# Attention with two expert layers: the two heads of a pair on even and odd partitions

## The chip, the cores and the metric

The kernel runs on one core of one Trainium2 chip. The metric is the device time of one execution in microseconds (us). The engines are TensorE (PE in the profile; PEld is its weight load), VectorE (DVE), ScalarE (ACT), GpSimd (POOL) and SyncE (SP). SP and ACT issue nearly all transfers of the stage that is told of here.

## What is computed

Attention of two kinds over 4 batches of 8 heads, 576 positions and 64 dimensions, then two layers of experts:

```python
q_d, k_d, v_d = (mean over 4 neighbouring positions of q, k, v)     # 144 pooled positions
out_d = softmax(q_d k_d^T / 8) v_d ; out_up = repeat(out_d, 4)
mask = abs(pos[:, None] - pos[None, :]) < 4                         # local attention, 7 keys wide
out_local = softmax(where(mask, q k^T / 8, -1e9)) v
x = out_up + out_local                                              # [2304, 512]
x = moe(x)          # top 1 of 8 experts, only rows with x @ w_skip > 0, plus x
x = moe2(x)         # noisy top 2 of 8 experts
```

## The kernel before

**Tiles of the attention stage.** The 2304 rows are cut into 18 tiles of 128 rows (4 groups of 32 queries). For each tile, class `Local` makes scores, softmax and values of the local attention; between the tiles, class `Pooled` does the same for the pooled attention of a batch. `push` (lines 1044 to 1083) runs a unit's `scores` and `soft`, the `turn` of the unit two back, the steps due now (`later`), then `exp`, and the `values` of the unit three back. The order on TensorE, ACT, VectorE and GpSimd is that of the program here (line 599); SP's queue is ordered by the framework.

**Heads in pairs.** The 8 heads go in 4 pairs. The two heads of a pair share the 128 partitions: queries `qT` hold head 0 in partitions 0 to 63 and head 1 in 64 to 127. The key tile `kT` has two blocks, `kT[:, 0]` and `kT[:, 1]`; head 0's keys fill partitions 0 to 63 of block 0, head 1's fill 64 to 127 of block 1, and the other halves are zero (`zero_keys`, line 631), so that one matmul gives both heads' scores (line 913). There are two key tiles, for even and odd batches. `load_qk` (728) loads a batch's keys, head 0 on SP and head 1 on ACT, then its queries on SP. `pool_qk` (737) sums groups of four keys and queries into `kd` and `qd`; the zero halves of `kd` are filled by `zero_pooled_keys`.

**Local exponentials and values.** `soft` (918) takes the maximum and writes scores minus maximum into `e` [128, 8 heads, 64 columns], of which 38 are used and column 48 holds 1e-9; `exp` works on it in place, `turn` transposes two heads at a time (128 columns) into `eT`, so the columns of head 0 come to partitions 0 to 63. `values` (938) sums `e` per head, multiplies `eT` with the window values `vw`, and scales. `load_local` (847) loads a tile's window values, 48 partitions per head, head 0 to partitions 0 to 47 on SP, head 1 to 64 to 111 on ACT.

**The head of the program** (1090 to 1106) makes masks, fills the first key tile (half on VectorE, half on GpSimd), loads batch 0's keys and queries, and for three tiles fills `e` (GpSimd) and `vw` (ACT) and loads window values; then `load_v(0)` loads the batch's values on SP. `start_1` (695), due at tile 0, fills the second key tile on ACT, ahead of tile 0's exponentials; `start_2` (707), at tile 1, loads batch 1; `start_3` makes the other constants. At tile 3 `load_wall` (1109) loads the gate weights on SP, four small transfers; one step later VectorE copies them into `wall`. The steps after it on VectorE stand behind that copy.

**After the stage** comes routing and the first expert layer (matmuls at lines 545 and 558), then the second (1520 and 1535).

Of the kernel before, what the change touches and what calls it, by code (L numbers as in the profile page):

```python
# [10 lines left out]
F32 = mybir.dt.float32  # L11
# [4 lines left out]
OP = mybir.AluOpType  # L16
AX = mybir.AxisListType

B, H, S, D = 4, 8, 576, 64
N = B * S  # L20
DM = H * D
# [3 lines left out]
NPOOL = S // 4  # L25
QUARTERS = S // 32
W = 38
WV = 48
# [70 lines left out]
def moe_attention_kernel(ctx, tc, q, k, v, w_skip, w_gate, w1, w2, g2, n2, noise, u1, u2, out, dbg=None):  # L99
# [22 lines left out]
    def bank(tag, shape, dtype=F32):  # L122
        return psums[0].tile(shape, dtype, name=tag, tag=tag, bufs=psum_bufs[tag])


    rt = ctx.enter_context(tc.tile_pool(name="routing", bufs=1))
    jp = rt.tile([128, 128], F32, name="jp", tag="rows")
# [11 lines left out]
    sel = consts.tile([128, 32], F32, name="sel")  # L139


    shared = ctx.enter_context(tc.tile_pool(name="shared", bufs=1))
    early_ctx = ctx.enter_context(ExitStack())
    ep = early_ctx.enter_context(tc.tile_pool(name="early", bufs=1, side="right"))
    V = nc.vector
# [451 lines left out]
    with ExitStack() as actx:  # L597
# [11 lines left out]
        for i in range(WARM):  # L609
            nc.tensor.matmul(wp, warm[:, 0:128], warm, start=True, stop=True)  # L610

        def load_v(b):
            t = ld.tile([128, 4, DM], F32, name="v0", bufs=NVG)
            u = ld.tile([64, DM], F32, name="v1", bufs=NVG)
            r0 = b * S * DM
            nc.sync.dma_start(t, v[r0:r0 + 512 * DM].rearrange("(p c d) -> p c d", p=128, d=DM))
            nc.sync.dma_start(u, v[r0 + 512 * DM:r0 + S * DM].rearrange("(p d) -> p d", d=DM))
            return t, u

        vws, vds, es, eps, kTs, kds = [], [], [], [], [], []  # L620
# [7 lines left out]
            else:  # L628
                e.memset(t, value)

        def zero_keys(i, e0, e1):
            t = shared.tile([128, 2, 4, S], F32, name=f"kT{i}", bufs=1, tag=f"shared{i}")
            kTs.append(t)
            fill(e0, t[0:64, 1])
            fill(e1, t[64:128, 0])

        def zero_pooled_keys(i, e0, e1):
            t = at.tile([128, 4, 2, NPOOL], F32, name=f"kd{i}", bufs=1)
            fill(e0, t[0:64, :, 1, :])
            fill(e1, t[64:128, :, 0, :])  # L640
            kds.append(t)

        def zero_values(e):
            t = at.tile([128, 2, 4, 4 * D], F32, name=f"vw{len(vws)}", bufs=1)
# [2 lines left out]

        def zero_exps(e):

            t = at.tile([128, 8, 64], F32, name=f"e{len(es)}", bufs=1)  # L650
            fill(e, t)
            e.memset(t[:, :, EPS:EPS + 1], 1e-9)
            es.append(t)

        def zero_pooled_exps(e):
# [37 lines left out]
        offsets = [tuple(window(4 * t + s)[3] for s in range(4)) for t in range(NT)]  # L693
        V, P, A = nc.vector, nc.gpsimd, nc.scalar
        def start_1():
            zero_keys(1, A, A)
            for n in range(3, NES):
                zero_exps(P)
            for n in range(3, NVW):
                zero_values(P)  # L700
            pooled_ones(P)
            zero_pooled_exps(P)
            zero_pooled_exps(P)
            for d in offsets:
                distances(d)

        def start_2():
            for n in range(2, NEP):
                zero_pooled_exps(P)
            zero_pooled_keys(1, P, P)  # L710
            pooled_ones(P)
            nc.gpsimd.dma_start(x_d[0:1], kTs[1][0:1, 1, 0, 0:DM + 16])
            load_qk(1)
            for n in range(1, NVG):
                vgs[n] = load_v(n)
            for t in range(3, NVW):
                load_local(t)
# [10 lines left out]
        def load_qk(b):  # L728

            held["k", b % 2] = b  # L730
            qT[b] = at.tile([128, 4, S], F32, name="qT", bufs=2)
            for g in range(2):
                r = slice(64 * g, 64 * g + 64)
                (nc.sync, nc.scalar)[g].dma_start(kTs[b % 2][r, g], k[b, r])
            nc.sync.dma_start(qT[b], q[b])

        def pool_qk(b, n):


            assert held["k", b % 2] == b  # L740
            held["kd", b % 2] = (b, n)
            if n == 0:
                qd[b] = at.tile([128, 4, NPOOL], F32, name="qd", bufs=2)
            kd, kT = kds[b % 2], kTs[b % 2]
            if n >= 8 and b in ONDVE:
                for i in range(n - 8, 4, 3):
                    o, x = kd[64:128, i, 1], kT[64:128, 1, i]
                    nc.vector.tensor_reduce(o, x.rearrange("p (g r) -> p g r", r=4), axis=AX.X, op=OP.add)
            elif n < 8:
                i = n // 2  # L750
                o, x = (qd[b][:, i], qT[b][:, i]) if n % 2 == 0 else (kd[0:64, i, 0], kT[0:64, 0, i])
                nc.vector.tensor_reduce(o, x.rearrange("p (g r) -> p g r", r=4), axis=AX.X, op=OP.add)
            else:
                o, x = kd[64:128, :, 1], kT[64:128, 1].rearrange("p a (g r) -> p a g r", r=4)
                nc.gpsimd.tensor_tensor(o, x[:, :, :, 0] if n == 8 else o, x[:, :, :, n - 7], op=OP.add)

        def pool_v(b, n):
# [89 lines left out]
        def load_local(t):  # L847

            vw = vws[t % NVW]
            for g in range(2):  # L850
                o = N * DM + (2 * t + g) * WV * 1024
                (nc.sync, nc.scalar)[g].dma_start(vw[64 * g:64 * g + WV, g],
                                  v[o:o + WV * 1024].rearrange("(p s c) -> p s c", s=4, c=256))

        def load_up(t):
# [40 lines left out]
        class Local:  # L896
# [21 lines left out]
            def soft(self):  # L918
                mx = at.tile([128, 8], F32, name="mx", bufs=NES)
                nc.vector.tensor_reduce(mx, self.p, axis=AX.X, op=OP.max)  # L920
                self.e = es[self.tile_no % NES]
                e = self.e[:, :, 0:W]
                nc.vector.tensor_tensor(e, self.p, mx[:, :, None].to_broadcast([128, 8, W]), op=OP.subtract)

            def exp(self):
                e = self.e[:, :, 0:W]
                nc.scalar.activation(e, e, AF.Exp, scale=1.0 / math.sqrt(D))
                self.sums = at.tile([128, 8], F32, name="sums", bufs=4)

            def turn(self):  # L930
                p = bank("pT", [128, 4, 128])
                for i in range(4):
                    nc.tensor.transpose(p[:, i, :], self.e[:, 2 * i:2 * i + 2, :].rearrange("p g c -> p (g c)"),
                                        ident)
                self.eT = at.tile([128, 4, 128], F32, name="eT", bufs=NET)
                nc.scalar.activation(self.eT, p, AF.Copy)

            def values(self):
                t = self.tile_no
                nc.vector.tensor_reduce(self.sums, self.e[:, :, 0:EPS + 1], axis=AX.X, op=OP.add)  # L940
                nc.vector.reciprocal(self.sums, self.sums)
                p = bank("pB", [128, 4, 2, D])
                for i in range(4):
                    for s in range(4):
                        nc.tensor.matmul(p[s * 32:s * 32 + 32, i, :, :], self.eT[:, i, s * 32:s * 32 + 32],
                                         vws[t % NVW][:, :, s, i * D:i * D + D], start=True, stop=True,
                                         tile_position=(0, 32 * s), skip_group_check=True)
                x = at.tile([128, DM + 16], F32, name="x", bufs=XB)
                xs[t] = x
                nc.vector.tensor_tensor(x[:, 0:DM].rearrange("p (h d) -> p h d", d=D),  # L950
                                        p.rearrange("p i g d -> p (i g) d"),
                                        self.sums[:, :, None].to_broadcast([128, 8, D]), op=OP.mult)
# [135 lines left out]
            return window(4 * t + 3)[0]  # L1088

        vgs = {}  # L1090
        for d in offsets[0:2]:
            distances(d)
        mask(offsets[0])
        zero_keys(0, V, P)
        load_qk(0)
        mask(offsets[1])
        for t in range(3):
            zero_exps(P)
            zero_values(A)
            load_local(t)  # L1100
        zero_pooled_keys(0, P, P)
        vgs[0] = load_v(0)

        nc.vector.memset(wall, 0.0)
        nc.vector.tensor_reduce(fours, ident.rearrange("p (c k) -> p c k", k=4), axis=AX.X, op=OP.add)
# [739 lines left out]
def laid_out(name, a):  # L1845

    import numpy as np

    if name in ("q", "k"):
        a = a.reshape(B, 4, 2, S, D).transpose(0, 2, 4, 1, 3).reshape(B, 128, 4, S)  # L1850
# [30 lines left out]
```

## Time and profile before

| | before |
|---|---|
| median of 3 runs | 811.86 us (809.7 to 814.34) |
| the profiled execution, whole | 807.94 us |
| its span, first to last instruction | 805.8 us |
| TensorE busy | 763.1 us (95%) |
| VectorE busy | 359.5 us (45%) |
| ACT busy | 256.8 us (32%) |
| GpSimd busy | 237.4 us (29%) |

Times in the rows count from the start of the span. "Idle before" and the bracket behind an instruction name what ended the idle time of its engine. A busy share is an average over stages that have different limits; the attention stage lasts up to about 160 us, the rest is the two expert layers.

### The profile page before, as it was taken

To read this page: it belongs to the slowest core of one execution; us is meant where nothing else is said; L and a number is where in the kernel's file an instruction comes from. 1 tells how busy PE (TensorE), PEld (TensorE's weight loads), DVE (VectorE), ACT (ScalarE), POOL (GpSimd) and SP (SyncE) were. 2 spreads that over 40 slices of the span, in tenths; PEclk is the share of its full clock that TensorE was granted. 3 is DMA by queue.
4 is the path that set the end of the run, shared out by engine and by line. 5 is a ranking of instruction groups with operands and counts; after the bars stand their busy time and mean duration, and the time that the engine had idled before them with its cause. 6 is when DMAs were issued, how large, how long until landed. Compare 5 with 4: busy or idle time off the path is not lost.

```text
span 805.8 us, 15250 instructions
## 1 busy us (share of the span) xinstructions
PE 763.1 (95%) x6265; PEld 673.7 (84%) x6265; DVE 359.5 (45%) x814; ACT 256.8 (32%) x491; POOL 237.4 (29%) x242
## 2 busy tenths in 40 slices
PE   4789998799999999998999999999999999999996
PEld 2467686699999989997899899898898898997984
DVE  4797788441101256554965434244243243243210
ACT  6245453211111204322433533334233343342211
POOL 8204522032122353203345502403404305102012
PEclk9899999599999999999999999999999999999999
DMA  9999666759788986224263843724625526424113
GB/s 224 239 258 248 198 179 185 244 160 372 286 312 296 328 317 202 58 80 81 71 180 106 225 114 119 173 73 131 146 71 161 108 84 165 110 79 70 17 13 47
DMA packets 61402, 131.55 MB, mean 163 GB/s; under 512 B 16097, under 2 KB 17136, under 8 KB 59792
## 3 DMA queue, kind: packets, MB, share of 16 engines
q1 hardware_dynamic: 32320, 59.05, 25.1%
q10 hardware_dynamic: 17024, 45.48, 16.5%
q0 software_dynamic: 11984, 25.98, 15.7%
q8 instruction: 52, 0.85, 0.5%
q14 instruction: 22, 0.18, 0.1%
HBM read 101.86 MB, written 23.91 MB: 156 GB/s over the span
## 4 chain that ended last, share of the span: by engine, by line
PE 75%; issue 1%; DMA 1%; POOL 0%; DVE 0%; ACT 0%; POOLq 0%; DVEq 0%; ACTq 0%
PE pH L1520 26%; PE pY L1535 26%; PE pH L545 9%; PE pY L558 8%; PE pT L1505 2%; PE pT L577 1%; PE pT L524 1%; PE pT L335 1%; DMA rows<-x_d,ixrg 1%; PE pH L566 0%; POOL out L306 0%; PE pH L582 0%; PE pT L212 0%; DVE w L1433 0%; ACT yo L1537 0%
## 5 line engine op out<-in xcount | busy, mean ns | idle before, releaser
L1535 PE MATMUL pY<-w,hh 128*128 128x512 f32 (+6 forms) x640 | 202.1, 397 | 0.0
L1520 PE MATMUL pH<-xh,w 128*128 128x256 f32 (+7 forms) x1024 | 195.3, 302 | 0.0
L1520 PEld LDWEIGHTS pH<-xh,w 128*128 128x128 f32 x1024 | 162.4, 188 | 1.0 <-DVE hl L1525 0.2
L1535 PEld LDWEIGHTS pY<-w,hh 128*128 128x128 f32 (+6 forms) x640 | 115.7, 184 | 27.3
L1196 DVE TENSOR_TENSOR w<-stg,w 128x1024 fp32r<-128x1024 f32 x64 | 82.9, 1302 | 107.0 <-ACT w L1195 106.9
L1535 PE MATMUL pY<-w,hl 128*128 128x512 f32 (+6 forms) x320 | 126.2, 394 | 0.0
L1520 PE MATMUL pH<-xl,w 128*128 128x256 f32 (+7 forms) x512 | 123.1, 301 | 0.0
L1525 DVE SCALAR_TENSOR_TENSOR hl<-pH,hh 128x256 fp32r<-128x256 f32 (+7 forms) x128 | 57.0, 474 | 129.2 <-ACT hh L1524 127.4
L306 POOL DMA_INDIRECT out<-yo,ix2w x35 | 67.5, 1929 | 130.1 <-ACT yo L1537 121.6
L1524 ACT ACTIVATE hh<-pH 128x256 fp32r<-128x256 f32 (+7 forms) x128 | 49.2, 424 | 149.7 <-PE pH L1520 145.9
L1520 PEld LDWEIGHTS pH<-xl,w 128*128 128x128 f32 x512 | 90.0, 188 | 0.0
L301 POOL DMA_INDIRECT rows<-x_d,ix2g x32 | 36.6, 1143 | 154.8 <-PE pT L1505 143.5
L1535 PEld LDWEIGHTS pY<-w,hl 128*128 128x128 f32 (+6 forms) x320 | 58.9, 184 | 15.2
L1195 ACT ACTIVATE w<-stg 128x1024 fp32r<-128x1024 f32 x64 | 67.1, 1055 | 9.6 <-DMA stg<-in_moe_w 9.6
L558 PE MATMUL pY<-hT,w 128*128 128x112 f32 (+7 forms) x512 | 69.2, 296 | 0.0
L558 PEld LDWEIGHTS pY<-hT,w 128*128 128x128 f32 x512 | 67.4, 190 | 0.2
L1537 ACT ACTIVATE yo<-pY,gt 128x512 f32<-128x512 f32 (+6 forms) x35 | 24.1, 687 | 136.5 <-PE pY L1535 71.8
L545 PE MATMUL pH<-xT,w 128*128 128x200 f32 (+6 forms) x448 | 66.2, 301 | 0.0
L545 PEld LDWEIGHTS pH<-xT,w 128*128 128x128 f32 x448 | 61.1, 190 | 1.8 <-issue 1.7
L306 POOL DMA_INDIRECT l_d<-x,ix1w x15 | 14.5, 965 | 92.4 <-DVE x L585 90.0
L560 DVE COPY yT<-pY 128x224 f32<-128x224 f32 (+7 forms) x16 | 7.5, 471 | 69.6 <-PE pY L558 69.6
L956 POOL TENSOR_TENSOR x<-x,up 128x512 f32<-128x512 f32 x16 | 21.3, 1335 | 47.0 <-DMA up<-od 29.8
(408 smaller groups left out, 860.2 us busy)
## 6 DMA issues: line engine op xcount, KB each, us to landing
w<-in_moe_w ACTq DMA_DIRECT2D x16, 2048.0 KB
stg<-in_moe_w SPq DMA_DIRECT2D x64, 512.0 KB, 3.4
x_d<-x SPq DMA_DIRECT2D x18, 264.0 KB, 2.3
qT<-in_q SPq DMA_DIRECT2D x4, 1152.0 KB
out<-zero ACTq DMA_DIRECT2D x3, 1536.0 KB, 8.6
v<-in_v SPq DMA_DIRECT2D x4, 1024.0 KB
up<-od SPq DMA_DIRECT2D x14, 256.0 KB, 5.5
vw<-in_v SPq DMA_DIRECT2D x18, 192.0 KB, 11.2
```

The lines of the kernel that those rows point to most:

```text
L301: return nc.gpsimd.indirect_dma_start(out=dst, out_offset=None, in_=x_d[0:n + 1], in_offset=bass.IndirectOffsetOnAxis(ap=idx, axis=0))
L306: return nc.gpsimd.indirect_dma_start(out=dst, out_offset=bass.IndirectOffsetOnAxis(ap=idx, axis=0), in_=src, in_offset=None, **kw)
L545: nc.tensor.matmul(self.p[:, j], w[:, k, f * 128:(f + 1) * 128], self.xT[:, k], start=k == 0, stop=k == KD - 1)
L558: nc.tensor.matmul(p[:, j], w[:, f, d * 128:(d + 1) * 128], self.hT[:, f], start=f == 0, stop=f == KF - 1)
L956: e.tensor_tensor(xs[t][:, 0:DM], xs[t][:, 0:DM], ups[t], op=OP.add)
L1195: nc.scalar.activation(hi[:, c], st[i], AF.Copy)
L1196: V.tensor_tensor(lo[:, c], st[i], hi[:, c].bitcast(F32), op=OP.subtract)
L1520: nc.tensor.matmul(p, w[:, k, fs], self.x[ch][n][:, k, 0:ch[1] - ch[0]], start=k == 0 and i == 0, stop=k == KD - 1 and i == 2)
L1524: nc.scalar.activation(hi, p, AF.Relu)
L1525: V.scalar_tensor_tensor(lo, p, 0.0, hi.bitcast(F32), op0=OP.max, op1=OP.subtract)
L1535: nc.tensor.matmul(p, h[:, f], w[:, f], start=f == 0 and i == 0, stop=f == KF - 1 and i == 2)
L1537: nc.scalar.activation(o, p, AF.Copy, scale=gate[0:n])
```

## The change

Keys, queries, exponentials, pooled keys and window values put head 0 of a pair on even partitions (or columns) and head 1 on odd ones. The key tile's blocks are now zeroed whole, before the keys land in them; the first key tile is filled at the program's head, and its `zero_keys` call goes. Pooling reads whole blocks (zeros too), so `zero_pooled_keys` goes. Queries are issued ahead of keys, batch 0's values move from SP to ACT behind the window values, and `load_qk(0)` comes before the masks. On the host, `q` is laid out with the dimension ahead of the head; `k` and `v` keep their layout in memory.

```diff
+    shared = ctx.enter_context(tc.tile_pool(name="shared", bufs=1))
+    kT0 = shared.tile([128, 2, 4, S], F32, name="kT0", bufs=1, tag="shared0")
+    nc.vector.memset(kT0[:, 0], 0.0)
+    nc.gpsimd.memset(kT0[:, 1], 0.0)
 ...
-        def load_v(b):
+        def load_v(b, e=nc.sync):
 ...
-            nc.sync.dma_start(t, v[r0:r0 + 512 * DM].rearrange("(p c d) -> p c d", p=128, d=DM))
+            e.dma_start(t, v[r0:r0 + 512 * DM].rearrange("(p c d) -> p c d", p=128, d=DM))
 ...
-        def zero_keys(i, e0, e1):
+        def zero_keys(i, e):
 ...
-            fill(e0, t[0:64, 1])
-            fill(e1, t[64:128, 0])
-
-        def zero_pooled_keys(i, e0, e1):
-            t = at.tile([128, 4, 2, NPOOL], F32, name=f"kd{i}", bufs=1)
-            fill(e0, t[0:64, :, 1, :])
-            fill(e1, t[64:128, :, 0, :])
-            kds.append(t)
+            fill(e, t[:, 0])
+            fill(e, t[:, 1])
+
+        def pooled_keys(i):
+            kds.append(at.tile([128, 4, 2, NPOOL], F32, name=f"kd{i}", bufs=1))
 ...
-            t = at.tile([128, 8, 64], F32, name=f"e{len(es)}", bufs=1)
+            t = at.tile([128, 4, 64, 2], F32, name=f"e{len(es)}", bufs=1)
 ...
-            zero_keys(1, A, A)
+            zero_keys(1, A)
 ...
+            nc.sync.dma_start(qT[b], q[b])
             for g in range(2):
-                r = slice(64 * g, 64 * g + 64)
-                (nc.sync, nc.scalar)[g].dma_start(kTs[b % 2][r, g], k[b, r])
-            nc.sync.dma_start(qT[b], q[b])
+                (nc.sync, nc.scalar)[g].dma_start(kTs[b % 2][g:128:2, g], k[b, 64 * g:64 * g + 64])
 ...
-                o, x = (qd[b][:, i], qT[b][:, i]) if n % 2 == 0 else (kd[0:64, i, 0], kT[0:64, 0, i])
+                o, x = (qd[b][:, i], qT[b][:, i]) if n % 2 == 0 else (kd[:, i, 0], kT[:, 0, i])
 ...
-                (nc.sync, nc.scalar)[g].dma_start(vw[64 * g:64 * g + WV, g],
+                (nc.sync, nc.scalar)[g].dma_start(vw[g:2 * WV:2, g],
 ...
-                e = self.e[:, :, 0:W]
-                nc.vector.tensor_tensor(e, self.p, mx[:, :, None].to_broadcast([128, 8, W]), op=OP.subtract)
+                nc.vector.tensor_tensor(self.by_head(W), self.p.rearrange("p (i g) w -> p i g w", g=2),
+                                        mx.rearrange("p (i g) -> p i g", g=2)[:, :, :, None].to_broadcast([128, 4, 2, W]),
+                                        op=OP.subtract)
+
+            def by_head(self, n):
+
+                return self.e.rearrange("p i c g -> p i g c")[:, :, :, 0:n]
 ...
-                    nc.tensor.transpose(p[:, i, :], self.e[:, 2 * i:2 * i + 2, :].rearrange("p g c -> p (g c)"),
+                    nc.tensor.transpose(p[:, i, :], self.e[:, i].rearrange("p c g -> p (c g)"),
 ...
-                nc.vector.tensor_reduce(self.sums, self.e[:, :, 0:EPS + 1], axis=AX.X, op=OP.add)
+                nc.vector.tensor_reduce(self.sums.rearrange("p (i g) -> p i g", g=2), self.by_head(EPS + 1), axis=AX.X,
+                                        op=OP.add)
 ...
         vgs = {}
+        kTs.append(kT0)
+        load_qk(0)
         for d in offsets[0:2]:
             distances(d)
         mask(offsets[0])
-        zero_keys(0, V, P)
-        load_qk(0)
         mask(offsets[1])
         for t in range(3):
             zero_exps(P)
             zero_values(A)
             load_local(t)
-        zero_pooled_keys(0, P, P)
-        vgs[0] = load_v(0)
+        pooled_keys(0)
+        pooled_keys(1)
+        vgs[0] = load_v(0, A)
```

## Rows read from the trace of the kernel before

**Rows 1.** The page: TensorE's busy share in 40 slices of the span, in tenths.

```profile
PE   4789998799999999998999999999999999999996
```

**Rows 2.** The chain that ended last: its first piece (start us, us, what).

```profile
171.80 5.61 PE pH L545 x48
```

**Rows 3.** VectorE's waits, 0 to 70 us (total us, times, longest).

```profile
DVE mx L920 <- PE pA L913: 9.6, 2, 9.1
DVE wall L1113 <- DMA gates<-in_moe_w_noise: 4.5, 1, 4.5
```

**Rows 4.** Busy us by stretch: PE, PEld, DVE, ACT, POOL, clock, DMA share, GB/s.

```profile
16.90:31.65 14.75, 11.42 (x165) 6.73 (x165) 14.05 (x27) 5.61 (x9) 4.01 (x36) 0.90 1.03 221
...
36.12:70.00 33.88, 29.95 (x477) 21.36 (x481) 31.47 (x75) 14.65 (x29) 7.77 (x7) 0.95 1.01 266
70.00:130.00 60.00, 58.01 (x1039) 45.32 (x1028) 44.67 (x126) 30.49 (x81) 18.08 (x14) 1.00 0.68 186
130.00:172.00 42.00, 34.15 (x343) 29.94 (x343) 27.06 (x112) 9.79 (x28) 9.71 (x9) 0.76 0.69 199
```

**Rows 5.** The same, by transfers: keys; batch values; narrow rows of values; later, weights.

```profile
3.00:6.00 3.00, 2.27 (x6) 0.60 (x4) 2.97 (x6) 2.53 (x2) 2.88 (x4) 1.00 0.97 209
...
15.00:16.00 1.00, 1.00 (x28) 0.53 (x23) 0.55 (x2) 1.00 (x1) 0.83 (x4) 1.00 0.95 393
17.00:19.00 2.00, 1.37 (x33) 0.96 (x32) 1.90 (x4) 1.98 (x2) 1.92 (x10) 1.00 1.14 157
...
180.00:200.00 20.00, 19.37 (x153) 18.71 (x152) 2.57 (x6) 3.14 (x7) 5.75 (x6) 1.00 1.03 365
```

**Rows 6.** Timeline of the head (start us, us, what, idle before).

```profile
2.90 2.01 POOL L629 MEMSET kT<- 64x2304 f32 x1
6.84 1.91 ACT L627 ACTIVATE vw<-zcol 128x2048 f32<-128x2048 f32 x1 [0.45 <-ACT vw L627]
14.05 1.24 PE L913 MATMUL pA<-kT,qT 128*32 128x76 f32 x32 [8.78 <-POOL ep L659]
14.36 4.27 ACT L627 ACTIVATE kT<-zcol 64x2304 f32<-64x2304 f32 x2 [5.62 <-DMA qT<-in_q]
18.66 0.81 ACT L927 ACTIVATE e<-e 128x304 f32<-128x304 f32 x2
23.87 1.08 PE L945 MATMUL pB<-vw,eT 128*32 128x128 f32 x32
30.10 0.69 DVE L950 TENSOR_TENSOR x<-pB,sums 128x512 f32<-128x512 f32 x1
```

**Rows 7.** Transfers from 0 to 20 us in 40 slices.

```profile
GB/s 0 0 0 0 240 424 221 166 277 184 129 276 276 203 111 295 258 258 350 254 225 365 170 274 311 221 254 344 213 336 295 492 328 303 172 127 172 158 98 158
```

**Rows 8.** Groups by shape (busy us, mean ns, idle before).

```profile
L752 DVE TENSOR_REDUCE qd<-qT 128x144 f32<-128x576 f32 x16 | 11.8, 738 | 0.0
L752 DVE TENSOR_REDUCE kd<-kT 64x144 f32<-64x576 f32 x16 | 11.7, 734 | 0.0
L940 DVE TENSOR_REDUCE sums<-e 128x8 f32<-128x392 f32 x18 | 9.9, 551 | 0.0
L923 DVE TENSOR_TENSOR e<-pA,mx 128x304 f32<-128x304 f32 x18 | 8.6, 475 | 0.8
L927 ACT ACTIVATE e<-e 128x304 f32<-128x304 f32 x18 | 8.2, 459 | 7.6 <-DVE e L923 7.6
L978 DVE COPY lg<-pW 128x25 f32<-128x25 f32 x18 | 3.2, 176 | 2.7 <-PE pW L977 2.7
L1106 DVE TENSOR_REDUCE sel<-ident 128x32 f32<-128x128 f32 x1 | 0.4, 351 | 0.0
L1113 DVE COPY wall<-gates 128x100 f32<-128x100 f32 x1 | 0.2, 249 | 4.5 <-DMA gates<-in_moe_w_noise 4.5
L1105 DVE TENSOR_REDUCE fours<-ident 128x32 f32<-128x128 f32 x1 | 0.2, 221 | 0.0
```

**Rows 9.** TensorE's waits, 36 to 130 us: the longest (total us, times, longest).

```profile
PE pB L945 <- DVE x L950: 3.3, 1, 3.3
```

More of the change, by code (lines that the diff above doesn't have):

```diff
@@ L139, in moe_attention_kernel @@
     sel = consts.tile([128, 32], F32, name="sel")
-    shared = ctx.enter_context(tc.tile_pool(name="shared", bufs=1))
     early_ctx = ctx.enter_context(ExitStack())
@@ L615, in load_v @@
             r0 = b * S * DM
-            nc.sync.dma_start(t, v[r0:r0 + 512 * DM].rearrange("(p c d) -> p c d", p=128, d=DM))
-            nc.sync.dma_start(u, v[r0 + 512 * DM:r0 + S * DM].rearrange("(p d) -> p d", d=DM))
+            e.dma_start(t, v[r0:r0 + 512 * DM].rearrange("(p c d) -> p c d", p=128, d=DM))
+            e.dma_start(u, v[r0 + 512 * DM:r0 + S * DM].rearrange("(p d) -> p d", d=DM))
             return t, u
@@ L648, in zero_exps @@
         def zero_exps(e):
-            t = at.tile([128, 8, 64], F32, name=f"e{len(es)}", bufs=1)
+            t = at.tile([128, 4, 64, 2], F32, name=f"e{len(es)}", bufs=1)
             fill(e, t)
-            e.memset(t[:, :, EPS:EPS + 1], 1e-9)
+            e.memset(t[:, :, EPS], 1e-9)
             es.append(t)
@@ L709, in start_2 @@
                 zero_pooled_exps(P)
-            zero_pooled_keys(1, P, P)
             pooled_ones(P)
@@ L746, in pool_qk @@
                 for i in range(n - 8, 4, 3):
-                    o, x = kd[64:128, i, 1], kT[64:128, 1, i]
+                    o, x = kd[:, i, 1], kT[:, 1, i]
                     nc.vector.tensor_reduce(o, x.rearrange("p (g r) -> p g r", r=4), axis=AX.X, op=OP.add)
@@ L750, in pool_qk @@
                 i = n // 2
-                o, x = (qd[b][:, i], qT[b][:, i]) if n % 2 == 0 else (kd[0:64, i, 0], kT[0:64, 0, i])
+                o, x = (qd[b][:, i], qT[b][:, i]) if n % 2 == 0 else (kd[:, i, 0], kT[:, 0, i])
                 nc.vector.tensor_reduce(o, x.rearrange("p (g r) -> p g r", r=4), axis=AX.X, op=OP.add)
             else:
-                o, x = kd[64:128, :, 1], kT[64:128, 1].rearrange("p a (g r) -> p a g r", r=4)
+                o, x = kd[:, :, 1], kT[:, 1].rearrange("p a (g r) -> p a g r", r=4)
                 nc.gpsimd.tensor_tensor(o, x[:, :, :, 0] if n == 8 else o, x[:, :, :, n - 7], op=OP.add)
@@ L921, in soft @@
                 self.e = es[self.tile_no % NES]
-                e = self.e[:, :, 0:W]
-                nc.vector.tensor_tensor(e, self.p, mx[:, :, None].to_broadcast([128, 8, W]), op=OP.subtract)
+                nc.vector.tensor_tensor(self.by_head(W), self.p.rearrange("p (i g) w -> p i g w", g=2),
[3 more added lines that the diff above has]
+                return self.e.rearrange("p i c g -> p i g c")[:, :, :, 0:n]
             def exp(self):
-                e = self.e[:, :, 0:W]
+                e = self.by_head(W)
                 nc.scalar.activation(e, e, AF.Exp, scale=1.0 / math.sqrt(D))
@@ L1849, in laid_out @@
     if name in ("q", "k"):
-        a = a.reshape(B, 4, 2, S, D).transpose(0, 2, 4, 1, 3).reshape(B, 128, 4, S)
+        a = a.reshape(B, 4, 2, S, D).transpose((0, 4, 2, 1, 3) if name == "q" else (0, 2, 4, 1, 3)).reshape(B, 128, 4, S)
     elif name == "v":
```

## The prediction

> **What bounds the kernel now.** I read the page first: TensorE is busy for 95% of the span, and its first two slices of 20 us have the digits 4 and 7 [rows 1]. The chain that ended last is TensorE work from 171.8 us on [rows 2]; nothing in the diff touches that part, so it can only start earlier. The change is all in the attention stage, so the next views are the waits of VectorE and the work by stretch. VectorE has two long waits there: 9.1 us for the first scores and 4.5 us for the last of the gate weights [rows 3]. Between them it works without a pause: 14.05 of 14.75 us from 16.9 to 31.65; then nothing of its own for 4.47 us; then 31.47 of 33.88 us to 70; after that TensorE is the bound, 58.01 of 60 us to 130 [rows 4]. Both waits end with a DMA. The DMA engines are busy for a share of 1.0 through all of this, yet move 209 to 266 GB/s [rows 4, 5]. Which transfers are slow shows where one kind runs alone: keys on 64 partitions per head, 209 GB/s; the whole-width batch of values, 393; 48- and 64-partition rows on one queue, 157 [rows 5]. The weights later run at 365 over 20 us, at the same busy share [rows 5]. So the head of the kernel, up to 36 us, is a stretch in which transfers that land on half of the partitions fill the DMA time, and VectorE is the next bound behind them.
>
> **The change part by part.**
>
> *First scores.* They wait for queries (1.18 MB) and two key halves (0.59 MB each), 2.36 MB. Before, they start at 14.05 [rows 6], with window values and the batch's values going between. After, queries are issued first, keys next, and the batch of values goes to ACT's queue behind three fills and three window loads, so 2.36 MB go nearly alone. Data starts at 2.0 us (four empty slices of 0.5) [rows 7]. Queries at 393 GB/s take 3.0 us, to 5.0. The keys newly wait for a fill of their whole block: one 2.0 us memset each on VectorE and GpSimd [rows 6], now from 0.8 to 2.8. It is covered, since the queue moves queries until 5.0; without that cover it would cost 2 us. How fast keys move on every second partition no row shows; the bounds are 209 and 393 GB/s, 5.6 and 3.0 us. I take 300 (3.9 us), nearer to the full width because the two sets together still write all partitions and each spans the whole range. Keys land at 8.9, first scores start near 9.2: 4.85 us earlier (10.9 and 8.3 at the bounds).
>
> The Trainium skill speaks on this in "SBUF — State Buffer", section Door 1: the partition number decides the port, partitions 0..63 reach half of the ports, 196 GB/s at 1 MiB against 328 for all 128, and two transfers to opposite halves gained only 6% over one. The 209 GB/s of the key pair agree [rows 5]. By its port formula even or odd partitions over the whole range reach every port; keys would take 3.6 us by its 328.
>
> *VectorE's own chain.* From the first scores to the end of the run at 31.65 it is 17.6 us. It holds the two softmax passes, pooling (0.734 us for 64 partitions, 0.738 for 128 [rows 8], so pooling whole blocks costs nothing) and the masks. With scores at 9.2 it ends at 26.8. Two things could hold it. The first exponential waits on ACT behind the fill of the second key tile (4.27 us): before it ran at 18.66, because ACT stood idle for 5.62 us ahead of that fill until the queries had landed [rows 6]. After, ACT makes its three value fills (1.91 us each [rows 6]) from about 3.4, with issues to 11.2 (the two moved value loads add some 1 us), then the key fill, and the exponential at 15.5. That is 3.1 us earlier, not 4.85, so TensorE's turn of the first tile is 1.7 us late against the scores. The batch of values, issued near 10.5 instead of 1.99, lands by about 19 (2.36 MB plus 1.18 each of window values, batch values and next queries, 5.9 MB, at about 340), where TensorE wants it at 18. VectorE first needs the result of either at its multiply, 30.10 before, whose matmuls were done at 24.95 [rows 6]: 5 us of slack, enough for both.
>
> *The gate weights.* Before, the last of them landed at 36.1, behind about 7.5 MB: first keys and queries, three tiles of window values, batch values, next keys and queries, a fourth tile. 3.93 MB of it are half-width. After: 3.93 MB at 300 take 13.1 us, 3.54 MB at 393 take 9.0, from 2.0 to 24.1, and 1.5 us for the small packets and landing: 25.6. VectorE asks at 26.8, so the 4.47 us go. The next keys newly wait for ACT's whole fill (to 15.5; before, they waited for no fill); on SP a window load and the gate weights stand behind them, on ACT the second exponential. The engines have 5.9 MB to move until about 17 to 19, so the late issue is covered. If it isn't, each microsecond of lateness beyond 26.8 comes off the gain. Sum at the copy of the gate weights: 36.12 to 26.8, 9.3 us. Next late is VectorE itself.
>
> *Interleaved exponentials.* Per tile one subtract writes them (0.475), one sum reads them (0.551), one ACT pass reads and writes them (0.459) [rows 8], 18 tiles, now at a step of 8 bytes. The nearest row reads at a step of 16 bytes: 0.249 us for 100 elements against 0.176 for 25 without a step [rows 8], 0.97 ns an element, and the unstepped sum has 1.4 [rows 8]: no cost, value zero. The other end is a step of 128 bytes, 0.351 against 0.221 us for 128 elements [rows 8], 1.0 ns each: 0.7 us per tile on VectorE, some 8 tiles while it is the bound, 5.6 us. For ACT no row has a step; its end is a doubling, 0.46 a tile, partly beside other work. I take 0.3 us for all. A gain there has no reason.
>
> *Edits with one answer.* The four pooled-key fills on GpSimd go, off the path. Transposes read the same 128 contiguous columns, matmul shapes stay, window values land on 96 partitions instead of 48 per half; after 36 us TensorE waits for none of them (its longest idle time there, 3.3 us, ends with VectorE [rows 9]), so faster loads bring nothing more.
>
> Total: 9.3 − 0.3 = 9.0 us. Profiled before: 807.94 (span 805.8 and 2.1 around it); the same execution after 798.9. The median before stands 3.9 above, so 811.86 − 9.0 = 802.9, said as 803.
>
> **Rivals.** (1) The step of two doesn't lift the rate; only the new order counts. First scores at 10.9; gate weights behind 3.93 MB at 209 (18.8) and 9.0: 31.3 with landing. Gain 4.8: 807. For it: each transfer still has 64 rows. Against: nothing in the rows but the full-width 393. The Trainium skill says on the same page, under "Can I just issue two DMAs to hit both halves?", that only one transfer spanning all 128 partitions reaches all ports; read strictly, that is this rival. (2) The head gains, but later stretches give half back: from 130 to 172 TensorE is busy 34.15 of 42 us at a granted clock of 0.76 [rows 4], and a later fall of the clock, or the transfers of pooled rows, can cost 3 to 5 us; 807. Against: everything there is released by earlier work, nothing by a fixed time. (3) The interleaved exponentials cost near their upper end: gain 3 to 4, 808. (4) Slower: partition-stepped rows move more slowly than now. The point is where the gate weights land after 36.12: 3.93 MB in 23.6 us, 166 GB/s. The slowest row is 157 [rows 5]: 25 us, 1.4 us late, and at half of 209 the gate weights land at 50, 13.8 us late, while 18 tiles of window values (7.1 MB) and keys (4.7 MB) would need 112 us: 813 to 826. Against: at 157 only 4 KB and 2 KB rows were moving, and the key rows of 9.2 KB never went below 209.
>
> **How the numbers follow.** Forecast 0.56 (799 to 806), rival 1 0.16, rival 2 0.13, rival 3 0.08, rival 4 0.07. A half per cent, about what a measurement here can tell from no change, is 4.1 us, or 807.8. Faster: 0.56, plus 0.21 of the 0.37 of rivals 1 to 3, which lie around that line: 0.77. Same: the other 0.16. Slower: 0.07. Range: fastest ends, keys at 393 and a few tenths of cold clock more, gain 13; slowest, rival 3 with a little: 798 to 810.
>
> **What would show it.** Right: first scores at 8.3 to 10.9; no wait of VectorE for gate weights; 250 to 390 GB/s while only keys move; the same durations of the stepped passes; the second matmul stage starting near 163 instead of 172. Wrong: the copy of the gate weights still waiting past 30 (the order on SP, or the rate), the multiply of the first tile waiting for ACT's late exponential, stepped passes longer by over 0.3 us, or a shift of 9 us at 36 that is gone at 172.

## The result and the profile after

Over four runs each on one chip, the changed kernel takes 800.35 us (798.93 to 801.14) and the kernel before 812.48 (809.7 to 814.34): a ratio of 0.9852, 95% interval 0.9819 to 0.9884. Two later series gave 0.9854 [0.9829, 0.988] and 0.9894 [0.9862, 0.9925]. The forecast of 803 (798 to 810) holds the time. The profiled execution took 801.14, its span 799.2, against 807.94 and 805.8 before: 6.8 us of the 12.1 between the medians, because the profiled execution of before was a quick one of its kernel and this one is a slow one of its own.

TensorE's line of the page after, 40 slices of the span, answers [rows 1]; the first slice is still poor:

```profile
PE   3999997999999999998999999999999999999996
```

The first piece of the chain that ended last (start us, us, what) answers [rows 2], 171.80 before:

```profile
163.54 5.61 PE pH L549 x48
```

VectorE's waits from 0 to 70 us after (total, times, longest) answer [rows 3]. The 4.5 us for the gate weights are gone, the wait for the first scores is 2.5 us shorter, and a wait of 1.8 us for the first values (`x`) is new:

```profile
DVE mx L919 <- PE pA L912: 7.4, 3, 6.6
DVE x L955 <- PE pB L950: 1.8, 1, 1.8
```

Busy time by stretch after (us, then PE, PEld, DVE, ACT, POOL, clock, DMA share, GB/s) answers [rows 4, 5]. In 3 to 6 us queries and the first keys move, in 6 to 9 the rest of the keys beside the next batch's queries; the DMA share is about 1 as before, but 402 to 409 GB/s go through:

```profile
3.00:6.00 3.00, 2.04 (x5) 0.73 (x6) 2.62 (x14) 1.85 (x2) 2.53 (x12) 1.00 1.00 409
...
6.00:9.00 3.00, 0.96 (x3) 0.15 (x1) 0.15 (x1) 2.17 (x2) 2.83 (x7) 1.00 1.00 402
...
36.00:70.00 34.00, 32.31 (x529) 23.66 (x519) 30.97 (x75) 16.69 (x36) 9.73 (x7) 1.00 0.75 238
70.00:130.00 60.00, 57.94 (x1052) 45.39 (x1050) 47.00 (x135) 30.52 (x78) 18.70 (x15) 1.00 0.67 198
130.00:163.00 33.00, 27.46 (x220) 24.54 (x220) 19.74 (x92) 6.73 (x22) 5.55 (x6) 0.74 0.66 206
```

The timeline of the head after (start us, us, engine, line, what, idle before and its releaser) answers [rows 6]; each engine's rows stand together:

```profile
0.73 0.41 SPq L732 DMA_DIRECT2D qT<-in_q  x1
3.28 0.61 SPq L734 DMA_DIRECT2D kT<-in_k  x1
3.94 0.56 SPq L732 DMA_DIRECT2D qT<-in_q  x1
...
9.43 1.91 ACT L631 ACTIVATE vw<-zcol 128x2048 f32<-128x2048 f32 x1 [0.59 <-ACT vw L631]
14.69 0.51 ACTq L851 DMA_DIRECT2D vw<-in_v  x1
15.24 1.46 ACTq L620 DMA_DIRECT2D v<-in_v  x1
16.74 0.51 ACTq L621 DMA_DIRECT2D v<-in_v  x1
17.30 4.13 ACT L631 ACTIVATE kT<-zcol 128x2304 f32<-128x2304 f32 x2 [5.97 <-DMA vw<-in_v]
21.34 0.46 ACT L931 ACTIVATE e<-e 128x304 f32<-128x304 f32 x1
...
11.48 1.24 PE L912 MATMUL pA<-kT,qT 128*32 128x76 f32 x32 [4.53 <-POOL dj L682]
...
21.95 1.08 PE L937 MATMUL pT<-ident,e 128*128 128x128 f32 x4 [6.14 <-ACT e L931]
...
29.16 0.69 DVE L955 TENSOR_TENSOR x<-pB,sums 128x512 f32<-128x512 f32 x1 [1.79 <-PE pB L950]
...
30.63 1.17 DVE L1119 COPY wall<-gates 128x100 f32<-128x100 f32 x1
```

Three things are to be seen. The second `qT` of SP, at 3.94, is the second batch's: SP's queue, which the framework orders, took it right behind the first batch's queries and keys. ACT's third window load is issued at 14.69, though the fill it needs ended at 11.34; behind it ACT stands idle for 5.97 us, and the first exponential, behind the key fill, comes at 21.34, later than the 18.66 of before. And the copy of the gate weights starts at 30.63, 5.5 us earlier than before.

The groups after by shape (busy us, mean ns, idle before) answer [rows 8]:

```profile
L751 DVE TENSOR_REDUCE kd<-kT 128x144 f32<-128x576 f32 x16 | 11.9, 744 | 0.0
...
L944 DVE TENSOR_REDUCE sums<-e 128x8 f32<-128x392 f32 x18 | 9.9, 551 | 0.0
...
L931 ACT ACTIVATE e<-e 128x304 f32<-128x304 f32 x18 | 8.7, 491 | 2.9 <-DVE e L921 2.8
L921 DVE TENSOR_TENSOR e<-pA,mx 128x304 f32<-128x304 f32 x18 | 8.6, 476 | 0.8
```

Since all kernels here run the same 6265 matmuls in the same order, the start of one matmul can be set against its start in the kernel before. The table has these shifts in us (negative is earlier), at six matmuls named by their start before. The first three columns are three profiled executions of the changed kernel; the others are the experiments below.

| start before | after | again | third | order alone | step alone | keys alone | values alone | fill first | queries held | both | both again | both, halves | fill shared |
|---|---|---|---|---|---|---|---|---|---|---|---|---|---|
| 14.05, first scores | −2.6 | −2.4 | −3.2 | −0.1 | +1.9 | −1.4 | −0.3 | −2.8 | −3.8 | −4.3 | −4.6 | −2.2 | −3.6 |
| 43.98 | −5.1 | −4.3 | −6.8 | −0.8 | −1.1 | −2.0 | −1.8 | −2.0 | −7.1 | −8.7 | −7.2 | −0.2 | −7.0 |
| 84.41 | −5.5 | −4.6 | −8.2 | +5.3 | −1.6 | −3.6 | +4.0 | −4.1 | −7.4 | −10.7 | −7.9 | +2.9 | −8.3 |
| 96.07 | −7.7 | −6.9 | −10.5 | +4.7 | −3.9 | −5.9 | +1.7 | −6.4 | −9.7 | −12.9 | −10.2 | +6.1 | −10.6 |
| 169.12, first expert layer | −8.3 | −7.8 | −11.2 | +3.6 | −5.1 | −7.1 | +1.6 | −8.4 | −10.8 | −14.7 | −11.9 | +4.0 | −11.1 |
| 798.08, end | −6.6 | −7.9 | −10.4 | +3.0 | −6.8 | −6.8 | +0.8 | −7.3 | −11.6 | −13.9 | −12.6 | +4.0 | −9.1 |

Three profiled executions of one kernel lie up to 3.4 us apart at 169, so a difference below that between two single profiles shows nothing by itself; medians and what a run did to a named wait carry the readings below.

### The profile page after: what moved, and what is told of

Its sections match the earlier page's. It is cut to its first block, busy times and chain, and to the rows that moved or that the text cites. A ratio compares the mean times of both kernels' runs of the same rounds, so it can differ in the third digit from the quotient of the medians.

```text
span 799.2 us, 15252 instructions
## 1 busy us (share of the span) xinstructions
PE 761.8 (95%) x6265; PEld 673.2 (84%) x6265; DVE 359.5 (45%) x814; ACT 257.7 (32%) x491; POOL 231.6 (29%) x238
## 4 chain that ended last, share of the span: by engine, by line
PE 74%; issue 2%; DMA 1%; POOL 1%; DVE 0%; ACT 0%; POOLq 0%; DVEq 0%; ACTq 0%
PE pY L1541 26%; PE pH L1526 25%; PE pH L549 9%; PE pY L562 9%; PE pT L1511 2%; PE pT L528 1%; PE pT L581 1%; DMA rows<-x_d,ix2g 1%; DMA rows<-x_d,ixrg 1%; PE pT L339 1%; PE pH L570 0%; POOL out L310 0%; PE pH L586 0%; PE pT L216 0%; POOL rows L305 0%
## 5 line engine op out<-in xcount | busy, mean ns | idle before, releaser
L562 PE MATMUL pY<-hT,w 128*128 128x112 f32 (+7 forms) x512 | 70.9, 300 | 0.0
L562 PEld LDWEIGHTS pY<-hT,w 128*128 128x128 f32 x512 | 69.1, 195 | 0.2
```

What stands on the lines that cost most here:

```text
L562: nc.tensor.matmul(p[:, j], w[:, f, d * 128:(d + 1) * 128], self.hT[:, f], start=f == 0, stop=f == KF - 1)
```

## The experiments

Times are medians; each ratio is to the kernel before, run in the same series.

| kernel | us (lowest to highest, runs) | ratio [95% interval] |
|---|---|---|
| first series, before | 807.41 (803.3 to 816.08, 25) | |
| order alone | 804.86 (801.78 to 810.76, 10) | 0.9962 [0.9934, 0.999] |
| step alone | 801.7 (800.63 to 804.49, 10) | 0.9921 [0.9894, 0.9948] |
| keys alone | 799.07 (798.77 to 800.99, 4) | 0.9877 [0.9835, 0.9919] |
| values alone | 805.42 (800.84 to 810.99, 10) | 0.9971 [0.9936, 1.0006] |
| second series, before | 810.41 (808.24 to 812.07, 7) | |
| changed kernel again | 798.36 (797.91 to 799.81, 4) | 0.9854 [0.9829, 0.988] |
| fill first | 799.21 (798.24 to 800.52, 4) | 0.9863 [0.9835, 0.989] |
| queries held | 796.32 (794.44 to 796.98, 4) | 0.9827 [0.9797, 0.9856] |
| both | 794.77 (794.03 to 800.66, 4) | 0.9836 [0.9791, 0.9881] |
| third series, before | 809.14 (804.6 to 814.53, 17) | |
| changed kernel, third | 800.79 (797.27 to 803.17, 6) | 0.9894 [0.9862, 0.9925] |
| both again | 797.59 (794.58 to 802.37, 6) | 0.9859 [0.9822, 0.9895] |
| both, on halves | 810.68 (807.76 to 816.17, 10) | 1.0025 [0.9995, 1.0055] |
| fill shared | 796.97 (795.77 to 798.76, 6) | 0.9843 [0.9815, 0.9872] |

### Rate or order: the change taken apart

Theory: the step of two lets the same transfers move faster. Rival: only the new order counts. Order alone is the changed kernel with every step of two undone (and the views and the queries' layout that belong to it):

```diff
-            t = at.tile([128, 4, 64, 2], F32, name=f"e{len(es)}", bufs=1)
+            t = at.tile([128, 4, 2, 64], F32, name=f"e{len(es)}", bufs=1)
 ...
-                (nc.sync, nc.scalar)[g].dma_start(kTs[b % 2][g:128:2, g], k[b, 64 * g:64 * g + 64])
+                (nc.sync, nc.scalar)[g].dma_start(kTs[b % 2][64 * g:64 * g + 64, g], k[b, 64 * g:64 * g + 64])
 ...
-                (nc.sync, nc.scalar)[g].dma_start(vw[g:2 * WV:2, g],
+                (nc.sync, nc.scalar)[g].dma_start(vw[64 * g:64 * g + WV, g],
```

> The changed kernel without any step of two: keys, queries, exponentials and window values lie on halves again; the new order stays (whole fills at the head, queries first, batch values on ACT). Theory of the rate: 3 to 6 us in the trace moves about 209 GB/s again once keys run, first scores at 12 to 14 us instead of 11.5, ratio to the kernel before 0.995 to 1.00. Theory of the order alone (the rival of the prediction): the order carries the gain, ratio 0.985 to 0.990.

Step alone keeps the layouts and takes back the order of the program: the first key tile filled at its old place, keys ahead of queries, batch 0's values on SP:

```diff
-            nc.sync.dma_start(qT[b], q[b])
             for g in range(2):
                 (nc.sync, nc.scalar)[g].dma_start(kTs[b % 2][g:128:2, g], k[b, 64 * g:64 * g + 64])
+            nc.sync.dma_start(qT[b], q[b])
 ...
-        vgs[0] = load_v(0, A)
+        vgs[0] = load_v(0)
```

> The step of two alone: keys ahead of queries, batch values on SP, first key tile filled where it was before. Theory of the rate: near 400 GB/s while keys and queries move, first scores at 11 to 13 us, and ACT not held so long ahead of the second key fill, ratio 0.983 to 0.990. Theory of the order alone: ratio 0.995 to 1.00.

Keys alone is the changed kernel with exponentials and window values back on halves, values alone the one with keys and queries back on halves; each takes its lines from the diff of order alone.

> The changed kernel with only keys and queries at the step of two; exponentials and window values on halves. If the head (first scores, gate weights) carries the gain, as the prediction had it: ratio 0.986 to 0.990, and the shift of TensorE's instructions against the kernel before is the same as in the changed kernel up to 44 us. If window values matter as much after 36 us: ratio 0.992 to 0.996, and the later steps of the shift are missing.

> The changed kernel with only exponentials and window values at the step of two; keys and queries on halves. If the head carries the gain through the keys: ratio 0.993 to 0.998, first scores at 12.5 to 14 us. If window values carry it: ratio 0.985 to 0.990.

The two stretches of order alone, columns as above, show the rate by itself. From 3 to 6 us mostly whole-width queries move, in both kernels at about 400, and not the 209 that was expected for this stretch. From 6 to 9 the keys move, in the changed kernel with the next queries beside them:

```profile
3.00:6.00 3.00, 2.04 (x5) 0.72 (x6) 2.62 (x14) 1.85 (x2) 2.53 (x12) 1.00 1.04 393
6.00:9.00 3.00, 0.95 (x3) 0.15 (x1) 0.14 (x1) 2.17 (x2) 2.83 (x7) 1.00 1.02 218
```

218 GB/s on halves, 402 with the step in the changed kernel, 399 in keys alone, 224 in values alone, at the same DMA share of 1.00 to 1.05 (356 to 362 in the later runs in which the gate weights' small packets move in this stretch). The rate is the step's, and of the keys' above all; one load of keys by itself is measured below, with both on halves.

Step alone is no clean opposite of order alone. The program's old order did not come back on SP, which issued the queries at 0.73, then the batch's values and the next queries, and the keys only at 5.00, behind the fill of their whole blocks. So no keys move there from 6 to 9 us, and its first scores (15.93 us, 11 to 13 expected) and its ratio (0.983 to 0.990 expected) say what the step is worth in that order of SP.

In time the order alone is worth 0.4%, the step alone 0.8%, the keys' step with the order 1.2%, the values' step with the order 0.3%, an interval that holds no change. The rival falls. Order alone's profile, of one of its slowest runs (810.7 us), shows where its gain goes: from 43.98 to 84.41 its shift goes from −0.8 to +5.3. TensorE stands there for 3.9 us at the transposes of batch values (L763, to 61.80), and after that stand its granted clock is 0.50, its lower level of 1.2 GHz, from 62 to 68. Values alone has this wait too (3.6 us), and both on halves (3.4, its row is shown below): all three have the new order and keys on halves. The kernel before has 0.8 us at the line of these transposes, the changed kernel none.

First scores and the copy of the gate weights came at 13.96 and 33.96 us in order alone, 15.93 and 35.80 in step alone, 12.64 and 33.75 in keys alone, 13.80 and 33.81 in values alone, against 11.48 and 30.63 in the changed kernel. Keys alone is thus 3 us behind it at the copy and 1.1 at 169.12, though up to 44 us the same shift was expected, and its ratio lies among the three of the changed kernel; how much of the head's gain reaches the end is not settled to better than such differences.

The Trainium skill's "SBUF — State Buffer", section Door 1, computes the port from the partition number; by it even partitions over the whole range reach all ports, and the rates agree with that. Under "Can I just issue two DMAs to hit both halves?" the same page says that only one transfer spanning all 128 partitions does; here two transfers of 64 rows, each at a step of two, moved at 399 to 402 GB/s together with whole-width queries, and one by itself at 374 (below), so the formula is to be followed and not that sentence.

### What held the head back: two waits in a row

The changed kernel once more, as the measure for the next three:

> The changed kernel once more, beside the next three on the same chip. Both theories expect a ratio of 0.983 to 0.989 to the kernel before, first scores at 11.3 to 11.7 us, the first exponential at 21 to 21.7 and the second matmul stage 7.5 to 8.5 us earlier than before; it says how far two profiled executions of one kernel lie apart.

Its ratio and scores came as expected. Fill first moves the second key tile's fill ahead of the third window load:

```diff
         def start_1():
-            zero_keys(1, A)
 ...
             zero_values(A)
+            if t == 2:
+                zero_keys(1, A)
             load_local(t)
```

> The changed kernel with the whole fill of the second key tile put ahead of the third window load on ACT, so that no DMA issue of ACT stands between the scores and the first exponential but for the batch values' own. Theory (ACT standing behind its DMA issues is what makes the first exponential late): the exponential at 16 to 19 instead of 21.3, TensorE's 6.1 us wait for it falls to 1 to 4, the copy of the gate weights at 27 to 29 instead of 30.6, the second matmul stage 1 to 2.5 us earlier than in the changed kernel, 798 to 800 us. Rival (the values of the batch, which land no sooner, or VectorE's own chain take its place): the exponential moves, the stage moves by under 0.5 us, 800 to 801.5.

The exponential came at 17.72 instead of 21.34, as the theory said, but the copy of the gate weights at 32.48 instead of 30.63 and the time stayed (799.21 beside 798.36): the rival was right. (799.21 lies in the theory's range, but only because the changed kernel itself came at 798.36 in this series and not near 801.) TensorE's waits to 40 us in this kernel show what took the place:

```profile
PE pA L911 <- DMA kT<-in_k: 4.3, 1, 4.3
...
PE pT L762 <- DMA v<-in_v: 3.1, 1, 3.1
PE pT L936 <- POOL fixed L173: 2.8, 1, 2.8
```

The wait for the exponential fell from 6.1 to 2.8 us, and one of 3.1 for batch 0's values is new; VectorE's wait for the first `x` grew to 3.9. The fill had moved ACT's issue of the values back to 16.52.

Queries held issues the second batch's queries from ACT, whose order is the program's:

```diff
-            nc.sync.dma_start(qT[b], q[b])
+            (nc.scalar if b == 1 else nc.sync).dma_start(qT[b], q[b])
```

> The changed kernel with the second batch's queries issued from ACT's queue at their place in the program instead of on SP at 3.9 us, between the first keys and the rest. Theory (these 1.18 MB between the first keys and the scores are what made the first scores 2.3 us later than forecast): first scores at 8.8 to 9.8 instead of 11.5, at about 400 GB/s. If the exponential on ACT decides behind them, the copy of the gate weights and the later stages move by under 0.7 us, 799.5 to 801.5; if the scores decide, they move by 1.5 to 2.5 us, 798 to 799.5. Rival (the two key halves themselves are slow): first scores stay within 0.5 us of 11.5.

First scores came at 10.22, later than the range by 0.4 but 1.26 earlier than in the changed kernel; the rival falls. The kernel is 2.0 us faster, and all its runs lie below those of the changed kernel. ACT's and TensorE's rows say why it is more than the scores' own 1.26 us:

```profile
10.72 1.91 ACT L631 ACTIVATE vw<-zcol 128x2048 f32<-128x2048 f32 x1 [1.88 <-DMA kT<-in_k]
12.66 0.52 ACTq L851 DMA_DIRECT2D vw<-in_v  x1
13.22 1.39 ACTq L620 DMA_DIRECT2D v<-in_v  x1
...
19.25 0.46 ACT L931 ACTIVATE e<-e 128x304 f32<-128x304 f32 x1
...
10.22 0.73 PE L912 MATMUL pA<-kT,qT 128*32 128x76 f32 x32 [3.26 <-POOL vd L670]
...
28.59 1.62 DVE L1119 COPY wall<-gates 128x100 f32<-128x100 f32 x1
```

With 1.18 MB less in front, ACT's third window load and the values are issued 2 us earlier too, so the exponential comes at 19.25. Both makes the two edits together:

> Both edits of the two runs before this one. If each is one of two waits in a row, neither alone shows the whole: first scores at 8.8 to 9.8, the exponential at 14.5 to 17, the copy of the gate weights at 26.5 to 28, the second matmul stage 2 to 4 us earlier than in the changed kernel, 796.5 to 798.5 us, which would be faster than both kernels. Rival (after the first 40 us TensorE is the bound of both and the head's gain is lost to the next wait for window values or weights): the stage moves by under 1 us, 799.5 to 801.

```profile
9.73 1.24 PE L911 MATMUL pA<-kT,qT 128*32 128x76 f32 x32 [2.78 <-POOL vd L667]
...
16.08 0.46 ACT L930 ACTIVATE e<-e 128x304 f32<-128x304 f32 x1
...
25.32 0.69 DVE L954 TENSOR_TENSOR x<-pB,sums 128x512 f32<-128x512 f32 x1
...
26.79 0.24 DVE L1120 COPY wall<-gates 128x100 f32<-128x100 f32 x1
```

From first scores to the copy it takes 17.06 us, with the first multiply unhindered: here VectorE's own chain is the bound of the head. The stage starts 6.5 us ahead of the changed kernel's, where 2 to 4 were expected. 794.77 us is 3.6 below the changed kernel of the series; the ratio, 0.9836, is no better than that of queries held, because one of the four runs took 800.66. To see whether that lead was scatter, both stood beside the changed kernel once more:

> The changed kernel for a third time, to stand on one chip and in the same rounds beside the next three. Expected by both theories: a ratio to the kernel before of 0.983 to 0.988, first scores near 11.5 us, the second matmul stage 7.5 to 8.5 us earlier than in the kernel before.

> The kernel with both edits (second batch's queries on ACT at their place, second key tile's fill ahead of the third window load) once more. Theory (the head was two waits in a row, and both are gone): 3 to 5 us below the changed kernel of the same rounds, ratio to the kernel before 0.978 to 0.982, first scores 9.5 to 10, no wait of VectorE for a DMA or for TensorE over 1 us between its first maximum and the copy of the gate weights. Rival (the lead of the first look was the scatter of single runs): within 1.5 us of the changed kernel.

The changed kernel's third series gave 0.9894, and its profile lay 2.9 to 3.4 us ahead of the two others at 169, both outside what was expected: the scatter is wider than the first two series showed. Both again is 3.2 us below it, as expected, but at 0.9859 instead of 0.978 to 0.982, and VectorE had a wait of 2.3 us for the first `x`, where none over 1 us was expected. A lead of 3.2 and 3.6 us in two series points to both as the faster kernel; the ranges and the intervals overlap, so this is not settled, and it is not shown to beat queries held alone.

Fill shared gives the second half of that fill to GpSimd:

```diff
             fill(e, t[:, 0])
-            fill(e, t[:, 1])
+            fill(nc.gpsimd, t[:, 1])
```

> Both edits, and the second half of the second key tile filled by GpSimd instead of ACT, so that the first exponential comes about 2 us sooner (13.8 to 14.8 instead of 16.1). Theory (VectorE's own chain of 17 us from the first scores is now the bound of the head, ACT no longer): the copy of the gate weights moves by under 0.7 us, the time stays within 1 us of the kernel with both edits. Rival (TensorE's 3.1 us wait for the exponential still decides): copy and stage 1.5 to 2 us earlier, 792.5 to 793.5 us where the kernel with both edits has 794.8.

The exponential came at 13.25, 2.5 us earlier than in both again, and the time is the same within 0.6 us: the exponential no longer decides, as the theory said. The two profiles are not quite alike, though: first scores came at 10.49 here, 1.1 us later than in both again. What decides is not VectorE's chain alone: TensorE stood for batch 0's values in its place (waits to 130 us):

```profile
PE pT L762 <- DMA v<-in_v: 5.3, 1, 5.3
```

### Is the step needed once the order is good?

Both on halves is both, with the lines of order alone taken over:

> Both edits, but no step of two at all: keys, window values and exponentials lie on halves as in the kernel before. Theory (the rate of the transfers is what the change sells, and the order pays only with it): 200 to 240 GB/s between 6 and 9 us, first scores 1.5 to 4 us later than with the step (11.3 to 13.5), the second matmul stage less than 4 us earlier than in the kernel before, ratio 0.99 to 1.0; the 1.5 to 1.9 us wait of TensorE at about 91 us that the kernel before has is there. Rival (with the better order the rate no longer matters, since the engines decide): ratio below 0.985, within 2 us of the kernel with the step.

It is no faster than the kernel before (1.0025 [0.9995, 1.0055]), 13 us behind both again; 228 GB/s between 6 and 9 us, first scores at 11.88, the stage 4.0 us later than before. The theory holds: the order pays next to nothing without the rate (order alone 0.4%, this kernel nothing). The two kernels have the same order on SP and ACT, so they also show the rate of keys by themselves: in a stretch in which ACT's key half is all that moves, but for small packets of 0.01 MB, first in both, then in both on halves:

```profile
7.25:8.25 1.00, 0.00 (x0) 0.00 (x0) 0.00 (x0) 1.00 (x1) 0.94 (x3) 1.00 0.91 374
```

```profile
8.25:10.25 2.00, 0.00 (x0) 0.00 (x0) 0.00 (x0) 0.38 (x1) 1.77 (x6) 1.00 0.97 194
```

One load of 64 rows moves at 374 GB/s at a step of two and at 194 in one half, at nearly the same DMA share. The waits of TensorE to 130 us in both on halves:

```profile
PE pA L911 <- DMA kT<-in_k: 4.9, 1, 4.9
...
PE pT L762 <- DMA v<-in_v: 3.7, 1, 3.7
PE pT L762 <- issue: 3.4, 1, 3.4
...
PE pT L965 <- ACT vd L764: 1.9, 1, 1.9
```

## Why the prediction was right, and where it was not

*Right: bound and sign.* The head was bound by transfers on half of the partitions, the step lifted their rate, and rivals 1, 3 and 4 fell: order alone gives 0.9962, the stepped passes cost next to nothing, and stepped rows moved at 374 GB/s, not below 166.

*VectorE's wait for the gate weights went, but not by the rate: the step that failed is "behind about 7.5 MB".* The prediction kept the gate weights behind the next keys and queries and let the faster rate bring them at 25.6. SP issued the last of them at 26.36 in the kernel before, behind those loads, but at 14.68 in the changed kernel, and ahead of the next keys in every other kernel here. So order alone, with every row on halves, has no such wait either. The kernel before, then order alone:

```profile
26.36 0.33 SPq L1112 DMA_DIRECT2D gates<-in_moe_w_noise  x1
```

```profile
17.85 0.43 SPq L1118 DMA_DIRECT2D gates<-in_moe_w_noise  x1
...
33.96 0.26 DVE L1119 COPY wall<-gates 128x100 f32<-128x100 f32 x1
```

Of the 5.5 us at the copy, order alone thus has 2.2 without any step.

*The rate was mis-sized.* It put 300 GB/s for keys; one key load by itself moved at 374, keys with queries at 402.

*First scores: the step that failed is "2.36 MB go nearly alone".* They came at 11.48, outside 8.3 to 10.9 although the keys moved faster than supposed. The second batch's queries went right behind SP's keys and took a share of the rate from ACT's half: by the trace's records of single transfers that half moved from 6.60 to 10.48, beside them. Held back, it was done at 9.22, 8.90 and 8.66 (queries held, both, both again), near the 8.9 of the prediction, and the scores came at 10.22, 9.73 and 9.43. So of the 2.28 us that were missing in the changed kernel 1.58 are the keys' landing, 10.48 instead of 8.9, and 0.7 are a second term: the prediction took 0.3 us from the landing to the scores, and from the last key row to the scores it was 1.0 there and 0.8 to 1.0 in these three. That SP's order is the framework's stood in the text; what it would do with a load whose tile is free was not asked.

*The first exponential: the step that failed is ACT's "issues to 11.2".* It was put at 15.5 and came at 21.34. The sum counted ACT's issues by their own time, and none of them as standing. The third window load was issued 3.3 us after its fill had ended, the value loads took 2 us behind it, and the key fill followed at 17.30. With the fill first and the queries held it came at 16.08 and 15.77. The kernel before had this wait already. Its third window fill ended at 8.75 [rows 6], and the load behind it came 5.25 us later:

```profile
14.00 0.32 ACTq L852 DMA_DIRECT2D vw<-in_v  x1
```

The prediction read ACT's 5.62 idle us there as the key fill waiting for the queries, and took them to be gone. The profile ends ACT's idle time with the landing of an earlier load each time (the queries before, window values after); why an issue stands there (room in the queue, or another wait) was not tried apart.

*"5 us of slack, enough for both" followed from that and fell too:* VectorE waited 1.79 us at that multiply. VectorE's own chain was right: 17.6 forecast, 17.06 in both, where nothing broke it, and 19.15 in the changed kernel with the wait.

*The head's sum* was 9.3; the copy started 5.5 us earlier, and the matmul at 43.98 5.1 (4.3 and 6.8 in the other two profiles).

*"After 36 us faster loads bring nothing more" was wrong, and made up for the head.* From 43.98 to 169.12 the shift grows by another 3.2 us (3.4 and 4.4 in the other two profiles), and 2.2 of it falls at one place, between 84 and 96. There the kernel before has this row:

```profile
91.48 0.63 PE L961 MATMUL pT<-ident,x 128*128 128x128 f32 x4 [1.85 <-ACT vd L766]
```

The changed kernel has no such wait. In order alone (1.5 us) and in both on halves (1.9 us), where nothing is stepped, it is there; in every kernel with a step in keys or values the shift falls by 2.2 to 2.3 us between those two matmuls. Ahead of it in the kernel before, the chain leads to ACT:

```profile
81.50 0.45 ACT L806 ACTIVATE ep<-ep 128x288 f32<-128x288 f32 x1
85.14 0.38 ACTq L852 DMA_DIRECT2D vw<-in_v  x1
85.57 0.60 ACT L814 ACTIVATE epT<-pT 128x512 f32<-128x512 f32 x1 [3.62 <-PE pA L913]
...
90.75 0.58 ACT L766 ACTIVATE vd<-pT 128x512 f32<-128x512 f32 x1
```

A window load issued at 85.14 stands between two passes of ACT that are 3.6 us apart, as in the head. That the wait depends on the step is shown; that this issue is its cause is only read from the rows. The prediction looked at TensorE's longest wait alone [rows 9] and took a wait that ends with an engine for one that no load had caused.

*Interleaved exponentials* were put at 0 to 0.3 us: on VectorE 551 and 476 ns against 551 and 475, on ACT 491 against 459, 0.03 us a tile. *Pooling whole blocks* is free, 744 ns against 734.

*The sum.* 9.0 was forecast and 8.26 found at the stage's entry (163.54, "near 163"), from a head that gave 4 us less and a later stretch that gave 3 more. So the time was met partly by two errors of opposite sign, which is luck. Between medians the gain was 12.13, 12.05 and 8.35 us in the three series, so the 9.0 is met no better than that. Rival 2, that later stretches give half back, was the wrong way round.

## What to carry to other kernels

Where transfers fill the DMA time at a low rate, look at which partitions their rows land on: 64 rows at a step of two moved 1.9 times as fast as the same rows in one half (374 against 194 GB/s), for no cost on VectorE. When loads are reordered, list for every queue what may now go ahead of the load that is waited for, and count an engine that issues loads as held until they are issued, not for the issue's own time. Two waits in a row can hide each other, so an edit that moves its own wait and gains no time, as fill first did, is worth a second try together with the other; that it gains then is not settled here.

## What was not expected of the hardware

The copy of the gate weights took 0.25 us before and 1.17 after, without waiting for data. It started while GpSimd was summing keys. Rows of the changed kernel, then of fill first, GpSimd's and VectorE's:

```profile
28.12 3.56 POOL L754 TENSOR_TENSOR kd<-kd,kT 128x576 f32<-128x576 f32 x2
```

```profile
28.65 3.50 POOL L753 TENSOR_TENSOR kd<-kd,kT 128x576 f32<-128x576 f32 x2
...
32.48 0.24 DVE L1120 COPY wall<-gates 128x100 f32<-128x100 f32 x1
```

In the first the copy ends at 31.80, 0.1 us after GpSimd's sums; in fill first it starts after them and takes 0.24. In the changed kernel's other two profiles, queries held, both again and fill shared it started beside such a sum and took 0.52 to 1.70 us; in both and in both on halves it came ahead of the sums and took 0.24. The Trainium skill's "SBUF — State Buffer", section "Who interferes with whom", says that a VectorE copy in a two-port mode and a GpSimd instruction shut each other out for a whole instruction; the nine copies named here agree. It costs up to 1.5 us at a place where VectorE is the bound.

The same kernel's median moved from 798.36 to 800.79 us between series, and that of the kernel before from 807.41 to 812.48, so the ratios, not the times, are to be compared across them.
